# Block copies on ScalarE, clearing by memset, an earlier first load of the MoE input, and the last stores in thirds

## The chip, the cores and the metric

The kernel runs on one core of a Trainium2 chip. The time is in device microseconds (us) for one execution. The engines are TensorE (PE, its weight loads are PEld), VectorE (DVE), ScalarE (ACT), GpSimd (POOL) and SyncE (SP). Here SP issues nearly all DMA transfers; a row "SPq" in the profile is one issue on SP's queue. Each engine works through its own list of instructions in order: an instruction that waits holds everything behind it on that engine. Each DMA issue also waits until the DMA eight issues earlier has landed, because the DMAs take turns on eight semaphores (named DMAHW0 to DMAHW7 below).

## The reference

Two computations follow each other. The first is a recurrence with a 40x40 state for each of 4 batches and 8 heads, over 768 tokens; the second is a gated network with a spatial matrix.

```python
for t in range(S):                                   # S = 768, D = 40, B = 4, H = 8
    y[:, :, t] = einsum('bhd,bhde->bhe', r_t, state)
    Sa = einsum('bhde,bhe->bhd', state, a_t)
    state = state * w_t[:, :, None, :] - einsum('bhd,bhe->bhde', Sa, b_t)
    state = state + einsum('bhd,bhe->bhde', v_t, k_t)
x = y.transpose(0, 2, 1, 3).reshape(B, S, 320)
h = maximum(x @ w_in, 0)                             # 320 -> 1024
u, v = h[..., :512], h[..., 512:]
v_n = (v - mean(v)) / sqrt(var(v) + 1e-6)
v_s = einsum('ts,bsd->btd', w_spatial, v_n) + b_spatial[None, :, None]
out = (u * v_s) @ w_out                              # 512 -> 320
```

## The kernel before, in words

Phase 1 is the recurrence in chunks of C = 64 tokens. There are 24 stages: two pairs of batches, each with 12 chunks. A stage works on eight units (`NU`: two batches by four pairs of heads), and the two heads of a pair lie in the two halves of the 128 partitions (`par`). In a chunk the recurrence needs the inverse of a unit triangular 64x64 matrix; this is built from inverses of its 32x32 diagonal blocks.

Preparation of a stage q, some stages ahead of its use: the inputs `ein` are loaded in pieces (L279), DVE makes two running products (`scan1`, `scan2`, L292 to L301) and the products `at` (L318) and `sl` (L324), ACT copies a column `sc` that SP stores to DRAM (`scr`, L312), and PE multiplies the 32x32 blocks (`lprime`, L339) into a PSUM tile `bk` (128 partitions by 256). `lblock` (L349) is a DVE product of that tile with the mask `maskl`, which holds -1 above the diagonal and 0 elsewhere; the result goes to a quarter of `Lc`. Four stages (`GS`) make a group. When its four quarters stand in `Lc`, the generator `invert` turns them with a DVE transpose into `A` (L357), writes ones on the diagonal (L359), runs 30 steps of a product and an addition (L363, L367), and transposes `A` twice (L372, L374) into the tiles that the stages use. The group's inversion is spread over the four stages ahead; the first one is done in one piece before the first stage.

A stage itself is a chain over PE and ACT with short DVE pieces: `c_bp` (PE L545, copied by ACT L555 into `Rt`), `c_ff` (PE L563, reads `Rt` with the tokens' columns that a load `Rt<-in_vtok`, L384, has put there), ACT's copy `ffs` (L571), `c_xx` (PE L581, ACT L592, then POOL's masking L406), the new state `Mc` (PE L619, DVE L630), and `c_y` (PE L641, DVE L654), whose result y is stored to the DRAM buffer `xs` after every second stage (SP L666). `c_bp` of the next stage needs `Mc`, and its bank is freed by DVE's y. Beside the chain, `b_lka`, `b_tok`, `b_l21`, `b_zt` and `b_h` prepare the next stage on PE and ACT (`tk` L457, `l` L477, `zt` L496).

From stage 10 on, the first matrix product of the network runs between the stages, 128 tokens of two batches at a time. `m_load` fetches them from `xs` with six transfers (SP L685, L689), `m_u` (PE L759) and `m_v` (PE L712) multiply, and ACT and DVE finish u and v (a tile `vr`, normalised on DVE), which go to the DRAM buffers `uts` and `vns`. Phase 2 loads them, applies the spatial matrix (`spatial`, PE L179 to L181) and multiplies with w_out (`proj`, PE L199): for each half of each batch, three tiles of 128 tokens are copied by ACT (L200) into `ot`, and SP stores `ot` (L201).

The order on each engine in phase 1 is a plan written by hand. `at(t, function, arguments)` puts a call at a time t in units of stages, the calls are sorted by t, and are issued in that order; the numbers in the tables decide which instruction stands ahead of which on an engine, and nothing is reordered later, until the last stage. From there a scheduler orders what is left.

Of the kernel before, what the change touches and what calls it, by code (L numbers as in the profile page):

```python
# [18 lines left out]
P = 128  # L19
C = 64  # L20
# [81 lines left out]
def phase2(ctx, tc, marks, vns, uts, wspT, bsp, wout, out):  # L102
# [86 lines left out]
    def proj(b, h, gh, gl):  # L189
        ot = stg.tile([P, TH // P, DO], F32, name="ot")  # L190
        for j in range(TH // P):
# [9 lines left out]
        nc.sync.dma_start(  # L201
            out=out[b, h * TH:(h + 1) * TH].rearrange("(j p) n -> p j n", p=P), in_=ot
        )
# [14 lines left out]
def phase1(ctx, tc, early, late, vtok, win, xs, vns, uts, dscr):  # L218
# [125 lines left out]
    def lblock(s):  # L344
        if s % GS == 0:
            st["Lc", s // GS] = inv.tile([P, GS * NU, HB], F32, name="Lc")
        Lc = st["Lc", s // GS]
        u0 = (s % GS) * NU
        nc.vector.tensor_tensor(  # L349
            out=Lc[:, u0:u0 + NU, :], in0=st.pop(("pl", s)),  # L350
            in1=maskl.unsqueeze(1).broadcast_to([P, NU, HB]), op=ALU.mult,
        )

    def invert(g):
        Lc = st.pop(("Lc", g))
        A = inv.tile([P, HB, HB], F32, name="A")
        nc.vector.transpose(out=A, in_=Lc.rearrange("p u t -> p t u"))  # L357
        yield
# [52 lines left out]
    def b_lka_out(s, par):  # L411
        At = st["blk", s][0]
        pk = st["pk", s]
        ev = PR[1 - par]
        if s in LKA_POOL:
            nc.scalar.activation(At[par][ev], pk[ev], AF.Copy)  # L416
            strict(At[par][ev], NU)
            return
        nc.vector.tensor_tensor(
            out=At[par][ev], in0=pk[ev],  # L420
            in1=maskp[ev].unsqueeze(1).broadcast_to([64, NU, C]), op=ALU.mult,
        )
# [12 lines left out]
    def b_h_out(s, par):  # L435
        ev = PR[1 - par]
        Rt = Rts[s % 2]
        if s in H_POOL:
            nc.scalar.activation(Rt[par][ev, :, 0:C], st["ph", s][ev], AF.Copy)
            strict(Rt[par][ev, :, 0:C], NU)  # L440
            return
        nc.vector.tensor_tensor(
            out=Rt[par][ev, :, 0:C], in0=st["ph", s][ev],
            in1=maskp[ev].unsqueeze(1).broadcast_to([64, NU, C]), op=ALU.mult,
        )
# [140 lines left out]
    def c_xx_out(s, g):  # L586
# [3 lines left out]
        if s in TRI_POOL:  # L590
            for par in range(2):
                done = nc.scalar.activation(Rt[par][PR[par], gp], xx[PR[1 - par]], AF.Copy, scale=-1.0)  # L592
            marks["a", s] = done.ins
            for par in range(2):
                strict(Rt[par][PR[par], gp, 0:C], NP)
            return
        for par in range(2):
            nc.scalar.activation(Rt[par][PR[par], gp, C:], xx[PR[1 - par], :, C:], AF.Copy, scale=-1.0)
        for par in range(2):
            ur, ev = PR[par], PR[1 - par]  # L600
            nc.vector.tensor_tensor(
                out=Rt[par][ur, gp, 0:C], in0=xx[ev, :, 0:C],
                in1=maskn[ev].unsqueeze(1).broadcast_to([64, NP, C]), op=ALU.mult,
            )
# [99 lines left out]
    def m_v(g, bq, i, k=0):  # L704
# [8 lines left out]
        vr = st["act"].tile([P, DH], F32, name="vr", bufs=2)  # L713
# [65 lines left out]
    H_POOL, LKA_POOL, TRI_POOL = range(0, 99), range(0, 99), range(0, 99)  # L779
# [47 lines left out]
    SCR, SLM = {4: 0.68}, {5: 0.83}  # L827
    PREP = {4: 0.03, 5: 0.45, 6: 1.03, 7: 1.45, 8: 2.03, 9: 2.45, 10: 3.03, 11: 3.45}
    for q in range(GS, NS):
        t = PREP.get(q, q - 8 + 0.01)  # L830
        at(t + 0.20, scan1, q)
        at(t + 0.28, scan2, q)
        at(SCR.get(q, t + 0.285), scr_store, q)
        at(t + 0.29, at_mul, q, AT_ENG)
# [191 lines left out]
```

## Time and profile before

| | |
|---|---|
| three runs | 665.67, 667.46, 667.48 us (median 667.46) |
| profiled execution | 665.08 us, its span 663.3 us |
| mean granted TensorE clock | 0.943 |
| busy: PE, DVE, ACT, POOL | 571.8, 448.4, 384.2, 225.9 us |
| share of the span | 86%, 68%, 58%, 34% |

The span is the time from the first to the last event of the profile; the execution's own time is 1.8 us more. In the profile a row of a group reads: line, engine, operation, what it writes and reads, shape, count, then busy time and mean length in ns, then the idle time of the engine just before, with what ended it. A row of the timeline begins with the start in us and the length; `x4` means four instructions in a row, and the bracket gives idle time before the row and what ended it. The first stage begins at about 54 us, and the last y is stored at 491.48 us, so a stage takes some 18 us in the mean.

### The profile page before, as it was taken

The page shows a single profiled execution, that of the slowest core. Times are in us where ns is not written, and L with a number is a line of the kernel's source. Part 1 is how long each engine was busy: PE and PEld are TensorE (multiplying, and loading weights), DVE is VectorE, ACT ScalarE, POOL GpSimd, SP SyncE. Part 2 cuts the span into 40 slices and gives each one's busy share as a digit, 9 for nine tenths or more (in the row PEclk, how much of TensorE's full clock was granted, in tenths as well). Part 3 has the DMA queues.
Part 4 walks back from the last instruction along what each step waited for, and adds up shares of the span by engine and source line. Part 5 has one row for each costly group of instructions (what it writes and reads, how often), then busy time and mean ns, then how long its engine had stood idle before and what let it go on. Part 6 is the DMA issues. An engine that isn't in the chain of part 4 may idle for free.

```text
span 663.3 us, 25848 instructions
## 1 busy us (share of the span) xinstructions
PE 571.8 (86%) x10960; PEld 518.3 (78%) x10960; DVE 448.4 (68%) x970; ACT 384.2 (58%) x860; POOL 225.9 (34%) x298
## 2 busy tenths in 40 slices
PE   1447885498777887999999999999989999999997
PEld 1437674487766776888888888888878999999997
DVE  8999789989999999488896677343384842332220
ACT  2135662377666775688878887888765543221212
POOL 6013330224332334144341332332354843352221
PEclk9967997789787898999999999999998999999999
DMA  8654778477555546657565365375395557150001
GB/s 199 121 107 67 134 152 147 70 175 155 135 127 115 131 117 120 142 127 172 154 190 148 86 173 144 90 198 132 89 262 182 162 155 240 61 157 31 31 31 59
DMA packets 106331, 87.68 MB, mean 132 GB/s; under 512 B 35496, under 2 KB 92072, under 8 KB 104296
## 3 DMA queue, kind: packets, MB, share of 16 engines
q1 hardware_dynamic: 105672, 84.31, 52.0%
q10 hardware_dynamic: 544, 1.72, 1.2%
q8 instruction: 86, 1.41, 1.0%
q14 instruction: 29, 0.24, 0.1%
HBM read 59.20 MB, written 20.50 MB: 120 GB/s over the span
## 4 chain that ended last, share of the span: by engine, by line
PE 63%; DVE 15%; DMA 7%; issue 6%; ACT 4%; SPq 3%; POOL 1%; DVEq 0%; ACTq 0%; POOLq 0%
PE po L199 6%; PE pv L759 6%; PE pv L712 6%; PE pg L179 5%; PE pg L180 5%; PE pg L181 5%; PE ch L563 4%; PE bp L545 4%; PE ch L581 4%; PE bk L429 2%; DMA ein<-in_early 2%; DVE itmp L363 2%; PE bk L451 2%; PE bk L399 2%; PE bp L641 2%
## 5 line engine op out<-in xcount | busy, mean ns | idle before, releaser
L406 POOL TENSOR_SCALAR_AFFINE_SELECT Rt<-Rt 64x512 f32<-64x512 f32 (+1 forms) x144 | 83.8, 584 | 156.2 <-ACT Rt L592 128.5
L406 POOL TENSOR_SCALAR_AFFINE_SELECT At<-At 64x512 f32<-64x512 f32 x48 | 41.5, 864 | 164.0 <-ACT At L416 151.9
L555 ACT ACTIVATE Rt<-bp 64x416 f32<-64x416 f32 x96 | 49.1, 511 | 56.2 <-PE bp L545 53.6
L363 DVE TENSOR_TENSOR itmp<-A 128x30 f32<-128x30 f32 (+9 forms) x180 | 66.5, 369 | 3.4
L179 PE MATMUL pg<-wsh,vh 128*128 128x384 f32 x192 | 65.4, 341 | 2.0 <-ACT vh L51 2.0
L545 PE MATMUL bp<-lin,Mc 40*64 40x104 f32 x768 | 47.3, 278 | 22.1 <-DVE y L654 19.8
L183 DVE TENSOR_TENSOR g<-pg,bb 128x384 f32<-128x384 f32 x32 | 17.8, 556 | 70.7 <-PE pg L181 68.4
L180 PE MATMUL pg<-wsl,vh 128*128 128x384 f32 x192 | 65.1, 339 | 0.0
L181 PE MATMUL pg<-wsh,vl 128*128 128x384 f32 x192 | 63.6, 339 | 0.0
L367 DVE TENSOR_TENSOR A<-A,itmp 128x30 f32<-128x30 f32 (+9 forms) x180 | 59.1, 328 | 6.2
L545 PEld LDWEIGHTS bp<-lin,Mc 40*64 40x64 f32 x768 | 40.7, 150 | 25.5 <-DVE y L654 22.7
L563 PE MATMUL ch<-Rt,At 128*64 128x104 f32 x768 | 48.0, 283 | 5.9 <-issue 4.8
L55 POOL TENSOR_TENSOR gl<-g,gh 128x384 fp32r<-128x384 f32 x32 | 33.0, 1035 | 58.1 <-ACT gh L51 58.1
L592 ACT ACTIVATE Rt<-ch 64x416 f32<-64x416 f32 x96 | 49.1, 511 | 4.6 <-PE ch L581 2.2
L563 PEld LDWEIGHTS ch<-Rt,At 128*64 128x64 f32 x768 | 42.2, 157 | 10.4 <-issue 7.1
L51 ACT ACTIVATE gh<-g 128x384 fp32r<-128x384 f32 x32 | 16.7, 521 | 54.3 <-DVE g L184 54.3
L339 PE MATMUL bk<-at,sl 64*32 64x32 f32 x1536 | 21.2, 203 | 26.5 <-DVE sl L324 20.7
L55 POOL TENSOR_TENSOR vl<-raw,vh 128x512 fp32r<-128x512 f32 x24 | 31.5, 1324 | 31.6 <-ACT vh L51 30.1
L581 PE MATMUL ch<-ffs,xf 64*64 64x104 f32 x768 | 41.7, 261 | 0.0
L339 PEld LDWEIGHTS bk<-at,sl 64*32 64x32 f32 x1536 | 17.7, 114 | 29.5 <-issue 14.4
L179 PEld LDWEIGHTS pg<-wsh,vh 128*128 128x128 f32 x192 | 36.6, 190 | 2.4 <-ACT vh L51 2.2
L630 DVE TENSOR_TENSOR Mc<-ch,scn 104x160 f32<-104x160 f32 x44 | 18.5, 436 | 29.0 <-PE ch L619 18.7
(132 smaller groups left out, 1497.8 us busy)
## 6 DMA issues: line engine op xcount, KB each, us to landing
ein<-in_early SPq DMA_DIRECT2D x108, 129.0 KB
lin<-in_late SPq DMA_DIRECT2D x48, 160.0 KB
At<-at SPq DMA_DIRECT2D x48, 128.0 KB
uts<-ur SPq DMA_DIRECT2D x48, 128.0 KB
vns<-vr SPq DMA_DIRECT2D x24, 256.0 KB
raw<-vns SPq DMA_DIRECT2D x24, 256.0 KB
ut<-uts SPq DMA_DIRECT2D x24, 256.0 KB
Rt<-in_vtok SPq DMA_DIRECT2D x48, 80.0 KB
```

Of the source, the lines that this page charges most:

```text
L55: eng.tensor_tensor(out=lo, in0=x, in1=hi.bitcast(F32), op=ALU.subtract)
L179: nc.tensor.matmul(pg, lhsT=vh[:, dc], rhs=w_h, start=(i == 0), stop=False)
L180: nc.tensor.matmul(pg, lhsT=vh[:, dc], rhs=w_l, start=False, stop=False)
L181: nc.tensor.matmul(pg, lhsT=vl[:, dc], rhs=w_h, start=False, stop=(i == NT - 1))
L363: nc.vector.tensor_tensor(out=tp, in0=A[:, k + 1:, k:k + 1].broadcast_to([P, m, k]), in1=A[:, k:k + 1, 0:k].broadcast_to([P, m, k]), op=AL ...
L367: nc.vector.tensor_tensor(out=A[:, k + 1:, 0:k], in0=A[:, k + 1:, 0:k], in1=tp, op=ALU.add)
L406: nc.gpsimd.affine_select(out=t, in_=t, pattern=[[0, k], [1, C]], base=0, channel_multiplier=-1, compare_op=ALU.is_gt, fill=0.0,)
L545: nc.tensor.matmul(bp[PR[par], q, :], lhsT=Mc[RR[par], n, :], rhs=li[RR[par], n, C:], start=(q == 0), stop=False, skip_group_check=True,)
L555: nc.scalar.activation(Rt[par][PR[par], gp, :], st["bp", g][PR[par]], AF.Copy)
L563: nc.tensor.matmul(ff[PR[1 - par], q, :], lhsT=At[par][:, n, :], rhs=Rt[par][:, n, :], start=True, stop=True,)
L581: nc.tensor.matmul(xx[ev, q, :], lhsT=xf[ev, n, :], rhs=ffs[ev, q, :], start=True, stop=True,)
L592: done = nc.scalar.activation(Rt[par][PR[par], gp], xx[PR[1 - par]], AF.Copy, scale=-1.0)
```

## The change

It has several parts.

- `lblock` is no longer a DVE product with a mask but an ACT copy of the whole block with the factor -1 (24 instructions change engine). The part that the mask would have made zero is now copied too. In `invert`, right after the transpose, five memsets write zeros over the upper half of all blocks of the group: halves of 16x16, then 8x8, 4x4, 2x2 and single elements. They run on DVE for group 0 and on POOL for the other five groups.
- The masks `maskl`, `maskp` and `maskn` and the code that makes them on POOL at the start are gone. Branches that were never taken are dropped.
- At the start, `scr_store(q)` comes right behind the scans of its stage; before, the four came in one piece behind the loads of `At` and `ein` (six transfers, since the first stage has none).
- The tables of the plan are written in another form, mostly with the same numbers. The earliest time of the first `m_load` becomes 9.92 instead of 10.12.
- `vr` has three buffers instead of two.
- In `proj`, each of the three tiles of a result is stored right behind its copy: 24 stores of 160 KB instead of 8 of 480 KB.

```diff
@@ proj
             nc.scalar.activation(ot[:, j, :], po, AF.Copy)
-        nc.sync.dma_start(
-            out=out[b, h * TH:(h + 1) * TH].rearrange("(j p) n -> p j n", p=P), in_=ot
-        )
+            t0 = h * TH + j * P
+            nc.sync.dma_start(out=out[b, t0:t0 + P], in_=ot[:, j, :])
...
@@ lblock
-        nc.vector.tensor_tensor(
-            out=Lc[:, u0:u0 + NU, :], in0=st.pop(("pl", s)),
-            in1=maskl.unsqueeze(1).broadcast_to([P, NU, HB]), op=ALU.mult,
-        )
+        nc.scalar.activation(Lc[:, u0:u0 + NU, :], st.pop(("pl", s)), AF.Copy, scale=-1.0)
@@ invert
-        A = inv.tile([P, HB, HB], F32, name="A")
+        Af = inv.tile([P, HB * HB + HB], F32, name="A")
+        A = Af[:, 0:HB * HB].rearrange("p (t s) -> p t s", s=HB)
         nc.vector.transpose(out=A, in_=Lc.rearrange("p u t -> p t u"))
+        h = HB // 2
+        while h:
+            x = Af.rearrange("p (b x) -> p b x", x=2 * h * (HB + 1))[:, :, h:h + h * HB]
+            (nc.gpsimd if g else nc.vector).memset(x.rearrange("p b (r c) -> p b r c", c=HB)[:, :, :, 0:h], 0.0)
+            h //= 2
         yield
...
@@ m_v
-        vr = st["act"].tile([P, DH], F32, name="vr", bufs=2)
+        vr = st["act"].tile([P, DH], F32, name="vr", bufs=3)
...
@@ the plan
-    T_DEC, T_MOE = 4.2, 11
+    T_DEC, T_MOE = (4.2, 5.2, 6.2, 7.2, 8.2, 9.2), 11
...
-        at(max(own[0] - 1.6, 2 * j + 2.1, T_DEC + 5.92), m_load, bq, i)
+        at(max(own[0] - 1.6, 2 * j + 2.1, T_DEC[5] + 7 * 0.1 + 0.02), m_load, bq, i)
...
@@ the start
-        p.memset(maskl, -1.0)
-        for q in range(P // HB):
-            rows = slice(q * HB, (q + 1) * HB)
-            p.affine_select(
-                out=maskl[rows], in_=maskl[rows], pattern=[[1, HB]], base=0,
-                channel_multiplier=-1, compare_op=ALU.is_gt, fill=0.0,
-            )
...
                 scan1(q, q)
                 scan2(q)
+            scr_store(q)
             at_mul(q, v)
...
         prep_load(4, 48)
-        for q in range(GS):
-            scr_store(q)
         b_lka(0)
```

Three places show what this does to the order. On SP, where y of the stages 8 and 9 is stored (`xs<-y`), the six loads of the first `m_load` (`xt<-xs`) stood behind it before:

```order
L279 DMA ein_121<-in_early 16x2064 [waits DMAHW3_49]
L666 DMA xs<-y_3731 40x4x128 [waits DMAHW4_49,DVE_49]
L666 DMA xs<-y_3731 40x4x128 [waits DMAHW5_49]
L666 DMA xs<-y_3736 40x4x128 [waits DMAHW6_49,DVE_49]
L666 DMA xs<-y_3736 40x4x128 [waits DMAHW7_49]
L279 DMA ein_121<-in_early 16x2064 [waits DMAHW0_49]
L534 DMA scn<-scr 64x320 [waits DMAHW1_49]
L534 DMA scn<-scr 64x320 [waits DMAHW2_49]
L392 DMA At_4140<-at 64x512 [waits DMAHW3_49,PE_49,Pool_49]
L279 DMA ein_121<-in_early 16x2064 [waits DMAHW4_49]
L685 DMA xt<-xs 128x2x128 [waits DMAHW5_49]
L689 DMA xt<-xs 64x128 [waits DMAHW6_49]
```

and in the changed kernel, from the same `ein` on:

```order
L275 DMA ein_121<-in_early 16x2064 [waits DMAHW3_49]
L662 DMA xt<-xs 128x2x128 [waits DMAHW4_49]
L666 DMA xt<-xs 64x128 [waits DMAHW5_49]
L666 DMA xt<-xs 64x128 [waits DMAHW6_49]
L662 DMA xt<-xs 128x2x128 [waits DMAHW7_49]
L666 DMA xt<-xs 64x128 [waits DMAHW0_49]
L666 DMA xt<-xs 64x128 [waits DMAHW1_49]
L643 DMA xs<-y_3737 40x4x128 [waits DMAHW2_49,DVE_49]
L643 DMA xs<-y_3737 40x4x128 [waits DMAHW3_49]
L643 DMA xs<-y_3742 40x4x128 [waits DMAHW4_49,DVE_49]
L643 DMA xs<-y_3742 40x4x128 [waits DMAHW5_49]
L275 DMA ein_121<-in_early 16x2064 [waits DMAHW6_49]
```

The loads now stand ahead of the y stores; they wait for earlier DMAs alone, while the stores wait for DVE. On ACT the block copies of the changed kernel take two places in a stage. In the stages 1 to 4 one stands between the two copies `tk`:

```order
L558 ACTIVATE ffs<-ch 128x416 x2
L444 ACTIVATE tk<-bk 128x320
L345 ACTIVATE Lc<-bk 128x256
L444 ACTIVATE tk<-bk 128x320
L753 ACTIVATE xf_127<-XT_556 128x8x32
```

and all later ones, and some of these stages too, ahead of the copies of `c_bp`:

```order
L510 ACTIVATE xf_128<-bk 32x8x32 x2
L345 ACTIVATE Lc<-bk 128x256
L542 ACTIVATE Rt_131<-bp_1666 64x416
L542 ACTIVATE Rt_132<-bp_1666 64x416
L542 ACTIVATE Rt_131<-bp_1685 64x416
L542 ACTIVATE Rt_132<-bp_1685 64x416
```

Nothing else moved on ACT in these rows; the copy is new there. On POOL the five memsets of group 1 stand between the masking of `At` and that of `Rt`:

```order
L405 AFFINE_SELECT At_1303<-At_1303 64x512
L355 MEMSET A 128x16x16
L355 MEMSET A 128x2x8x8
L355 MEMSET A 128x4x4x4
L355 MEMSET A 128x8x2x2
L355 MEMSET A 128x16
L405 AFFINE_SELECT Rt_129<-Rt_129 64x4x64
```

The memsets wait for the group's transpose on DVE. Of DVE's instructions only the transposes at the end of the inversion wait for the memsets.

More of the change, by code (lines that the diff above doesn't have):

```diff
@@ L254, in phase1 @@
     eseg = ends.rearrange("p (n c) -> p n c", c=WSEG)
-    maskl = const.tile([P, HB], F32, name="maskl")
     ident = const.tile([P, P], F32, name="ident")
-    maskp = const.tile([P, C], F32, name="maskp")
-    maskn = const.tile([P, C], F32, name="maskn")
     Mc = const.tile([P, NU, C], F32, name="Mc")
@@ L414, in b_lka_out @@
         ev = PR[1 - par]
[L415 to L421, printed above, removed]
-        )
+        nc.scalar.activation(At[par][ev], pk[ev], AF.Copy)
+        strict(At[par][ev], NU)
     def b_h(s):
@@ L437, in b_h_out @@
         Rt = Rts[s % 2]
[L438 to L445, printed above, removed]
+        nc.scalar.activation(Rt[par][ev, :, 0:C], st["ph", s][ev], AF.Copy)
+        strict(Rt[par][ev, :, 0:C], NU)
     def b_tok(s, h):
@@ L589, in c_xx_out @@
         xx = st["xx", g]
[L590 to L596, printed above, removed]
         for par in range(2):
-            nc.scalar.activation(Rt[par][PR[par], gp, C:], xx[PR[1 - par], :, C:], AF.Copy, scale=-1.0)
+            done = nc.scalar.activation(Rt[par][PR[par], gp], xx[PR[1 - par]], AF.Copy, scale=-1.0)
+        marks["a", s] = done.ins
         for par in range(2):
[L600 to L604, printed above, removed]
+            strict(Rt[par][PR[par], gp, 0:C], NP)
     def c_mp(s, g):
@@ L778, in phase1 @@
     AT_ENG, SL_ENG, LO_ENG, XC = v, v, p, act_copy
-    H_POOL, LKA_POOL, TRI_POOL = range(0, 99), range(0, 99), range(0, 99)
     M1, M2, M3, M4 = 0.22, 0.46, 0.65, 0.80
@@ L852, in phase1 @@
         for k in range(8):
-            at(T_DEC + i + k * 0.10 - (0.9 if k == 0 else 0), step, gen)
-    at(T_DEC + 5.9, open_act)
+            at(T_DEC[i] + k * 0.1 - (0.9 if k == 0 else 0), step, gen)
+    at(T_DEC[5] + 7 * 0.1 + 0.01, open_act)
     slots = [T_MOE + k // 4 + (M1, M2, M3, M4)[k % 4] for k in range(3 * NS)]
@@ L890, in phase1 @@
         pads(v, ein[1])
-        p.memset(maskl, -1.0)
-        for q in range(P // HB):
-            rows = slice(q * HB, (q + 1) * HB)
-            p.affine_select(
-                out=maskl[rows], in_=maskl[rows], pattern=[[1, HB]], base=0,
-                channel_multiplier=-1, compare_op=ALU.is_gt, fill=0.0,
-            )
         pads(p, ein[2])
@@ L905, in phase1 @@
         make_identity(nc, ident)
-        for m, val in ((maskp, 1.0), (maskn, -1.0)):
-            p.memset(m, val)
-            for rows in PR:
-                p.affine_select(
-                    out=m[rows], in_=m[rows], pattern=[[1, C]], base=0,
-                    channel_multiplier=-1, compare_op=ALU.is_gt, fill=0.0,
-                )
         for t in (Mc, *xfs):
```

28 lines of the change are left out of this document (15 added, 13 removed).

## The prediction

> **What bounds the kernel now.** I read the table of stretches first, because the 68% of DVE and 86% of PE in the page's first part average over stages with different limits. Its columns are the stretch and its length, then busy time of PE, PEld, DVE, ACT and POOL, then granted TensorE clock, DMA share and GB/s.
>
> ```profile
> 14.00:54.00 40.00, 18.09 (x453) 16.48 (x455) 37.07 (x82) 11.45 (x28) 4.17 (x6) 0.77 0.59 110
> 54.00:84.60 30.60, 26.64 (x822) 23.26 (x818) 22.94 (x32) 19.90 (x48) 12.61 (x14) 0.91 0.68 116
> 84.60:147.00 62.40, 42.02 (x1214) 37.06 (x1208) 57.78 (x113) 32.17 (x75) 14.78 (x22) 0.84 0.69 134
> 147.00:257.00 110.00, 90.45 (x2604) 79.92 (x2606) 106.02 (x215) 77.54 (x176) 38.52 (x53) 0.91 0.57 129
> 257.00:264.00 7.00, 2.46 (x30) 1.93 (x26) 6.72 (x14) 2.69 (x7) 2.14 (x2) 0.77 0.95 129
> 264.00:366.00 102.00, 101.45 (x2368) 88.82 (x2366) 77.91 (x183) 80.31 (x185) 33.79 (x51) 0.98 0.61 154
> ```
>
> From 14 to 54 DVE is 37.07 of 40 us busy (scans, then the whole inversion of group 0). From 54 to 84.6 no engine is full. From 84.6 to 257 DVE is 163.8 of 172.4 us busy: it is the bound, and every DVE operation taken out there is worth its own length. From 257 to 264 PE works 2.46 of 7 us. After 264 PE is 99% busy, and nothing taken from DVE can pay. The waits of 54 to 135 (total, times, longest) say the same: PE's c_bp stands still for y on DVE.
>
> ```profile
> PE bp L545 <- DVE y L654: 8.3, 2, 4.5
> ```
>
> **The 24 block copies (L349) go from DVE to ACT.** On DVE one takes 0.42 us; ACT's nearest copies out of the bank, larger and narrower than the new 128x256, are the next two rows.
>
> ```profile
> L349 DVE TENSOR_TENSOR Lc<-bk,maskl x24: 410/419/426, 14.7 to 351.3; 128x256 f32<-128x256 f32 x24
> L457 ACT ACTIVATE tk<-bk 128x320 f32<-128x320 f32 x48 | 19.7, 435 | 8.0 <-PE bk L451 7.6
> L477 ACT ACTIVATE l<-bk 32x256 f32<-32x256 f32 x48 | 18.0, 375 | 8.3 <-PE bk L468 7.4
> 140.96 0.42 DVE L349 TENSOR_TENSOR Lc<-bk,maskl 128x256 f32<-128x256 f32 x1 [0.94 <-PE bk L339]
> 147.07 0.44 DVE L630 TENSOR_TENSOR Mc<-ch,scn 104x160 f32<-104x160 f32 x1 [1.40 <-ACT Rt L592]
> ```
>
> I take 0.40 us on ACT. Twelve of the 24 copies, those of stages 7 to 18, lie between 84.6 and 257, and DVE starts its next operation about 0.34 us after one. Five of them come before 147.07, 5 x 0.34 = 1.7 us (the fifth, at 140.96, had DVE wait 0.94 us for PE too). But there Mc waited 1.40 us for ACT's Rt, so what DVE wins only lengthens this wait, unless the work of PE and ACT ahead of it moves forward too. It does in part, since PE's c_bp waits for DVE's y; against it ACT has a copy of 0.40 us more, between two tk copies. I take 1.0. The next six stand in gapless DVE work: 6 x 0.34 = 2.1 us (the twelfth comes behind the y that counts below). Together **-3.1 us** by 257. Bounds: 5 (twelve copies at 0.34 and the wait of 0.94) and nothing (each 0.34 us turns into a wait for a load). In 54 to 84.6 I count none: three copies lie there, but DVE then waits for loads or stores, as at 84.63, right behind the last.
>
> ```profile
> 84.63 1.26 DVE L292 TENSOR_TENSOR_SCAN S<-ein,ends 128x528 f32<-128x528 f32 x1 [0.96 <-DMA scr<-sc]
> 297.72 2.12 ACT L555 ACTIVATE Rt<-bp 64x416 f32<-64x416 f32 x4 [1.34 <-PE bp L545]
> ```
>
> After 264 the copy stands ahead of Rt<-bp on ACT. At 297.72 ACT had waited 1.34 us for PE's c_bp, and on PE the lprime matmuls that fill the bank stand ahead of that c_bp: the copy fits into this idle time. Price there 0; without that cover 0.40 us for each of five copies.
>
> **The clearing memsets.** Nothing in the trace has their strided shape. They clear 256, 128, 64, 32 and 16 elements a partition; the rows bracket them by size:
>
> ```profile
> L881 DVE MEMSET ein<- 128x512 f32 x1 | 0.5, 485 | 0.0
> L359 DVE MEMSET A<- 128x32 f32 x6 | 0.5, 85 | 0.0
> L881 POOL MEMSET ein<- 128x512 f32 x2 | 1.0, 522 | 0.1
> L907 POOL MEMSET maskp<- 128x64 f32 x1 | 0.1, 146 | 0.0
> ```
>
> A line through the DVE rows gives about 0.27, 0.17, 0.11, 0.09 and 0.07: 0.7 us for group 0, on DVE (bounds 0.4 and 2.4, five times each end). On POOL the five make about 0.9 us (0.7 to 2.6), behind the group's transpose. They hold only POOL's next affine_select, and DVE's last transposes, some 20 or more us later. At the second group's transpose POOL is idle:
>
> ```profile
> 94.01 0.49 POOL L406 TENSOR_SCALAR_AFFINE_SELECT Rt<-Rt 64x256 f32<-64x256 f32 x1 [5.08 <-ACT Rt L592]
> 25.56 0.42 DVE L349 TENSOR_TENSOR Lc<-bk,maskl 128x256 f32<-128x256 f32 x1 [0.44 <-PE bk L339]
> 26.02 1.94 DVE L357 STREAM_TRANSPOSE A<-Lc 128x1024 f32<-128x1024 f32 x1
> ```
>
> At the start two earlier copies leave DVE's way to the last lprime (2 x 0.34 us); the transpose at 26.02 then starts about 0.6 us earlier, and the memsets give 0.7 back: **0** (-0.6 to +1.8). The scr stores moved ahead, and At and ein(4) moved behind six of them, lie under the inversion, which holds all to 54; the mask building that POOL loses lies ahead of it. The dropped branches were never taken.
>
> The Trainium skill has a rule that bears here: SBUF — State Buffer, "Who interferes with whom", says that a DVE instruction with two SBUF inputs collides with a GpSimd instruction that reads SBUF, not with one that only writes. By it the memsets cost the inversion steps beside them nothing, and the sum stays; without it, 0.9 us of memsets in each of five groups could stretch DVE by up to 4.5 us, and the sum would be that much poorer. No run so far shows a memset beside a step.
>
> **The first loads of xs (m_load) move up on SP.** Now SP stands before xs<-y(9) until DVE has y, 236.47 to 241.44, and only behind it come six xt loads.
>
> ```profile
> 235.40 1.07 SPq L279 DMA_DIRECT2D ein<-in_early  x2
> 241.44 1.56 SPq L666 DMA_DIRECT2D xs<-y  x4
> 246.20 0.41 SPq L685 DMA_DIRECT2D xt<-xs  x1
> 249.84 1.12 SPq L689 DMA_DIRECT2D xt<-xs  x2
> 257.08 0.58 SPq L384 DMA_DIRECT2D Rt<-in_vtok  x1
> 258.05 0.52 PE L759 MATMUL pv<-xh,wl 128*128 128x256 f32 x3
> 261.99 0.58 PE L563 MATMUL ch<-Rt,At 128*64 128x104 f32 x2 [3.42 <-issue]
> 263.68 3.00 PE L563 MATMUL ch<-Rt,At 128*64 128x104 f32 x30 [1.12 <-DMA Rt<-in_vtok]
> 257.08 6.47 DMA Rt<-in_vtok
> ```
>
> From 241.44 SP issues without a pause to the second vtok at 257.08; it lands 6.47 us later, at 263.55, and c_ff(11), which could start at about 258.57, runs only then: 5.1 us. The six loads take 246.20 to 250.96, 4.76 us of SP. In the change they stand ahead of xs<-y(9), and wait for earlier DMAs alone, so they fall into SP's idle 4.97 us. Everything behind, vtok included, is issued about 4.7 us earlier: **-4.6 us** (bounds -5.1, the whole wait, and 0, if landing is what limits: the DMA share of 257 to 264 is 0.95). It adds to the 3.1 because SP's row starts from ein issues that wait for DVE to free their buffer; if it didn't, both together would give 4.7.
>
> **PE's clock behind that wait.** The next rows have the columns of the first table.
>
> ```profile
> 264.00:265.00 1.00, 1.00 (x16) 1.00 (x14) 1.00 (x1) 0.00 (x0) 0.00 (x0) 0.50 0.68 177
> 268.00:270.00 2.00, 2.00 (x50) 1.82 (x50) 0.00 (x0) 1.18 (x4) 0.00 (x0) 1.00 0.42 96
> 243.68 1.92 PE L563 MATMUL ch<-Rt,At 128*64 128x104 f32 x32
> ```
>
> The granted clock is 0.50 behind the idle time and 1.00 again at 268. Thirty matmuls of c_ff take 3.00 us there, where 32 took 1.92 at 243.68. A short wait would save this 1.2 us; I take **-1.0** (0 to -1.7).
>
> The Trainium skill, TensorE: Matmul & The Clock Gate, "Part 1: The HAM clock gate (the "warmup" mystery)", says that an idle window of about 3.4 us halves the clock, and as long a busy one restores it. The trace agrees: 3.42 us of idle, then 0.50 until 268. No row shows the shortest wait that costs the clock; by the rule the term is -1.2 for a wait under 3.4 us, and 0 for one above it.
>
> **Third vr buffer.** At 489.89 ACT's vr waits 0.75 us for the store of an older vr, and 1.95 us of PE hang behind.
>
> ```profile
> 489.89 0.60 ACT L714 ACTIVATE vr<-itmp 128x512 f32<-128x512 f32 x1 [0.75 <-DMA vns<-vr]
> 498.57 0.44 PE L179 MATMUL pg<-wsh,vh 128*128 128x384 f32 x1 [1.95 <-ACT vh L51]
> ```
>
> Between them stand SP's stores and loads (xs<-y, raw<-vns), so I pass on half of the 0.75: **-0.4** (0 to -1.95).
>
> **The stores in thirds.** Every proj result is stored as three pieces, 24 issues instead of 8. SP waits there for ACT (81.2 us, below), so the 16 added issues of 0.37 us cost nothing. Only the last store counts.
>
> ```profile
> SPq L201 <- ACT ot L200: 81.2, 6, 17.3
> 659.26 0.44 ACT L200 ACTIVATE ot<-po 128x320 f32<-128x320 f32 x1 [1.32 <-PE po L199]
> 659.72 0.37 SPq L201 DMA_DIRECT2D out_y<-ot  x1
> 660.80:661.20 0.40, 0.00 (x0) 0.00 (x0) 0.00 (x0) 0.00 (x0) 0.00 (x0) 1.00 1.01 358
> ```
>
> At 358 GB/s 480 KB move in about 1.4 us and a third in 0.47: **-0.95** (0 to -1.1).
>
> The Trainium skill speaks against splitting: DMA: Bandwidth & Descriptors, "Anatomy of one DMA — SWDGE (gpsimd) path", gives 2.0 us plus bytes over 436 GB/s for each DMA. As an estimate the last third then takes 2.4 us against 3.1, a gain of 0.75; the sum would be 0.2 us poorer, since the first two pieces go out beside PE's work. The row gives 3.6 us from issue at 659.72 to the end of the span at 663.3.
>
> **The sum.** -3.1 - 4.6 - 1.0 - 0.4 - 0.95 = -10.05 us. The terms hang in one chain of due times, and what one frees may meet the next wait, so I keep 9 of the 10. The profiled execution took 665.08 us (span 663.3): 656.1. The runs' median, 667.46, is 2.4 above it, so I forecast **658.5**.
>
> **The rivals.** (A) The transfer is hidden no better: vtok is issued earlier, but lands late since DMA is full (share 0.95). Against it: the six loads leave the crowded time for one in which SP now issues nothing. Then -3.1 - 0.4 - 0.95 = -4.45: **663.0**. (B) DVE's gain turns into waits for loads on SP's row, and vtok stays: only the tail is left, -1: **666.5**, the same. For it speaks 54 to 84.6; against it DVE's 96% in 147 to 257. (C) Slower: ACT becomes what the stage loop waits for. Its copies stand in order ahead of Rt<-bp, tk and ffs; if lprime on PE ends later than c_bp, ACT is held with Rt<-bp ready behind it, and PE with it. Price: 20 copies behind the start x 0.40 = 8.0, less the 1.35 of tail and vr, +6.6: **674**. It decides from the point where ACT's wait for c_bp is under 0.40 us; now it is 0.56 a copy in the mean (53.6 us over 96, below), but most comes in few long waits. ACT is 79% busy from 264 to 366 and gets to about 81%.
>
> ```profile
> L555 ACT ACTIVATE Rt<-bp 64x416 f32<-64x416 f32 x96 | 49.1, 511 | 56.2 <-PE bp L545 53.6 <-POOL xl L55 0.7 <-issue 0.2
> ```
>
> **How the numbers follow.** Forecast 0.58, A 0.24, B 0.11, C 0.07. A measurement here tells about 0.3%, 2.0 us, from no change. The forecast and A lie beyond that bound: faster 0.82, same 0.11, slower 0.07. The likeliest's own range is 654 (the best bounds of the two large terms and the clock, -13.2) to 661 (DVE's term at nothing, -7); with A and 2 us above it the range becomes **654 to 665**, leaving out B and C.
>
> **What would show it.** Right: no L349-like operation on DVE; the waits of PE's c_bp for y shorter; the DVE-bound stretch shorter by 3 us; the six xt issues ahead of xs<-y(9); vtok issued near 250, c_ff(11) waiting under 2 us and a clock of 1.00 behind it; the span's end 2.7 us behind the last ot. Wrong: ACT Lc holding Rt<-bp with PE waiting (C); vtok's landing over 8 us after its issue (A); new DVE waits for ein or scr (B).

## The result, and the profile after

The changed kernel took 662.52 us (median of 16 runs, 658.51 to 667.07), the kernel before 667.19 us (16 runs on the same chip, 660.87 to 669.38). The ratio is 0.9948 with a 95% interval of 0.9926 to 0.9971: **3.5 us faster (1.9 to 4.9), where 9.0 were forecast.** The medians lie 4.7 us apart and the means 3.5 (666.25 and 662.75); the ratio and its interval are those of the means. The direction was right; the size was less than half of the forecast.

One profiled execution of each hides this. That of the changed kernel took 664.58 us (span 662.9), that of before 665.08: half a microsecond apart, the one above its kernel's median, the other below. Runs of one kernel spread by more than 8 us here, so the ratios below come from many runs, and what a profile shows is read in several.

The table of stretches of the changed kernel, with the columns of the prediction's first one:

```profile
14.00:54.00 40.00, 18.27 (x454) 16.48 (x444) 36.31 (x83) 12.76 (x32) 3.98 (x6) 0.86 0.61 109
54.00:84.60 30.60, 26.81 (x702) 23.53 (x698) 20.76 (x27) 20.09 (x49) 11.72 (x14) 0.80 0.73 111
84.60:147.00 62.40, 41.02 (x1165) 36.72 (x1160) 52.77 (x101) 29.32 (x68) 12.73 (x23) 0.78 0.58 119
147.00:257.00 110.00, 91.45 (x2506) 80.31 (x2508) 103.49 (x201) 80.69 (x185) 36.67 (x60) 0.89 0.64 136
257.00:264.00 7.00, 5.50 (x212) 4.74 (x214) 6.66 (x19) 4.98 (x11) 5.34 (x8) 1.00 0.89 142
264.00:366.00 102.00, 101.94 (x2350) 89.64 (x2348) 81.84 (x186) 83.58 (x192) 36.32 (x60) 0.98 0.62 155
```

From 84.6 to 257 DVE is now 156.3 us busy of 172.4, against 163.8 before. The window is fixed in time, so this says only that DVE idles more. The work itself did not come earlier: y(9), the y of stage 9, ended at 248.18 us, against 241.75 before (247.7 and 244.0 in a second profile of each). The groups of the changed kernel name the wait (the transposes and copies of all six groups, then the memsets):

```profile
L351 DVE STREAM_TRANSPOSE A<-Lc 128x1024 f32<-128x1024 f32 x6 | 11.7, 1951 | 11.3 <-ACT Lc L345 11.3
L345 ACT ACTIVATE Lc<-bk 128x256 f32<-128x256 f32 x24 | 9.2, 382 | 19.1 <-PE bk L335 18.9
L355 DVE MEMSET A<- 128x256 f32 x1 | 0.3, 272 | 0.1
L355 DVE MEMSET A<- 128x16 f32 x1 | 0.1, 72 | 0.0
L355 POOL MEMSET A<- 128x256 f32 x5 | 1.6, 312 | 26.9 <-DVE A L351 26.9
```

A copy takes 0.382 us on ACT (0.40 forecast), and the memsets cost what was worked out (0.27 to 0.07 us on DVE). But DVE stands 11.3 us ahead of the six transposes, waiting for ACT's copies; before, the transposes waited 0.2 us in all, and the products ahead of them 5.5 us for PE (the same groups of the kernel before):

```profile
L357 DVE STREAM_TRANSPOSE A<-Lc 128x1024 f32<-128x1024 f32 x6 | 11.8, 1964 | 0.2
L349 DVE TENSOR_TENSOR Lc<-bk,maskl 128x256 f32<-128x256 f32 x24 | 10.1, 419 | 5.5 <-PE bk L339 5.5
```

In the timeline of the changed kernel the second and third group have most of it. Below the two transposes stand ACT's copies ahead of them, and PE's lprime ahead of the first of these copies:

```profile
95.16 1.95 DVE L351 STREAM_TRANSPOSE A<-Lc 128x1024 f32<-128x1024 f32 x1 [5.23 <-ACT Lc L345]
148.34 1.97 DVE L351 STREAM_TRANSPOSE A<-Lc 128x1024 f32<-128x1024 f32 x1 [3.47 <-ACT Lc L345]
94.75 0.38 ACT L345 ACTIVATE Lc<-bk 128x256 f32<-128x256 f32 x1 [0.54 <-PE bk L335]
147.93 0.38 ACT L345 ACTIVATE Lc<-bk 128x256 f32<-128x256 f32 x1
93.58 1.08 PE L335 MATMUL bk<-at,sl 64*32 64x32 f32 x64
```

The profile names ACT, but most of this is a wait for PE. For the second group lprime ends at 94.66, and ACT, which had been idle for 0.54 us, copies at 94.75. For the third group lprime ends at 146.98, and ACT comes to the copy 0.95 us later, behind `ffs` and a `tk`. Over all six groups 7.8 of the 11.3 us pass before lprime has ended and 3.5 behind it. Other profiles agree on the second part only: with all copies in these places on ACT, DVE waits 7.7 to 11.3 us in five profiles, 3.3 to 4.5 of it behind lprime; with the product on DVE it waits 5.1 to 11.1 us in five, for PE. So what is new is ACT's part, some 3 to 4 us, and the pair of profiles shown here makes the rest look larger than it is.

The loads of `xs` and vtok, on SP and PE of the changed kernel:

```profile
243.06 0.43 SPq L662 DMA_DIRECT2D xt<-xs  x1
245.33 2.07 SPq L666 DMA_DIRECT2D xt<-xs  x2
247.87 1.86 SPq L643 DMA_DIRECT2D xs<-y  x4
258.47 0.59 SPq L383 DMA_DIRECT2D Rt<-in_vtok  x1
268.33 1.65 PE L550 MATMUL ch<-Rt,At 128*64 128x104 f32 x32
```

All six loads are issued by 247.40, ahead of the y stores. vtok is issued 10.6 us behind the y stores' start, against 15.6 before: the move does what it should. c_ff(11) no longer waits for it (the last row has no wait), and the clock from 257 to 264 is 1.00. At the end, SP's last store and ACT's last copy:

```profile
659.74 0.44 ACT L200 ACTIVATE ot<-po 128x320 f32<-128x320 f32 x1 [1.32 <-PE po L199]
660.20 0.33 SPq L202 DMA_DIRECT2D out_y<-ot  x1
```

The span ends 2.69 us behind the last copy (660.18), against 3.65 before.

### The profile page after: what moved, and what is told of

Read it like the earlier page. It is cut to its first block, busy times and chain, and to the rows that moved or that the text cites. A ratio compares the mean times of both kernels' runs of the same rounds, so it can differ in the third digit from the quotient of the medians.

```text
span 662.9 us, 25888 instructions
## 1 busy us (share of the span) xinstructions
PE 577.4 (87%) x10960; PEld 523.0 (79%) x10960; DVE 445.2 (67%) x951; ACT 394.3 (59%) x884; POOL 225.2 (34%) x312
## 4 chain that ended last, share of the span: by engine, by line
PE 67%; DVE 13%; issue 7%; ACT 5%; DMA 5%; SPq 2%; POOL 1%; DVEq 0%; ACTq 0%; POOLq 0%
PE po L199 6%; PE pv L736 6%; PE pv L689 6%; PE pg L179 5%; PE pg L181 5%; PE pg L180 5%; PE bp L532 5%; PE ch L550 4%; PE ch L568 4%; PE bk L422 3%; PE bk L438 3%; DVE itmp L362 3%; PE bk L398 3%; DMA ein<-in_early 3%; DVE A L366 2%
## 5 line engine op out<-in xcount | busy, mean ns | idle before, releaser
L362 DVE TENSOR_TENSOR itmp<-A 128x30 f32<-128x30 f32 (+9 forms) x180 | 68.7, 382 | 3.5
L532 PE MATMUL bp<-lin,Mc 40*64 40x104 f32 x768 | 47.7, 280 | 16.7 <-DVE y L631 14.2
L51 ACT ACTIVATE gh<-g 128x384 fp32r<-128x384 f32 x32 | 16.7, 522 | 54.5 <-DVE g L184 54.5
L568 PE MATMUL ch<-ffs,xf 64*64 64x104 f32 x768 | 43.2, 267 | 0.0
L568 PEld LDWEIGHTS ch<-ffs,xf 64*64 64x64 f32 x768 | 38.3, 144 | 1.1
```

Of the source, the lines that this page charges most:

```text
L362: nc.vector.tensor_tensor(out=tp, in0=A[:, k + 1:, k:k + 1].broadcast_to([P, m, k]), in1=A[:, k:k + 1, 0:k].broadcast_to([P, m, k]), op=AL ...
L532: nc.tensor.matmul(bp[PR[par], q, :], lhsT=Mc[RR[par], n, :], rhs=li[RR[par], n, C:], start=(q == 0), stop=False, skip_group_check=True,)
L568: nc.tensor.matmul(xx[ev, q, :], lhsT=xf[ev, n, :], rhs=ffs[ev, q, :], start=True, stop=True,)
```

## The experiments

All ratios are against the kernel before on the same chip in the same batch; the changed kernel has 0.9948 in two batches.

| kernel | ratio | 95% interval |
|---|---|---|
| block part alone | 0.9979 | 0.9947 to 1.0011 |
| first m_load alone | 0.9962 | 0.9932 to 0.9991 |
| stores in thirds and third vr alone | 0.9978 | 0.9953 to 1.0003 |
| changed, block part undone | 0.9936 | 0.9905 to 0.9966 |
| before, DVE product three times | 1.0160 | 1.0123 to 1.0197 |
| changed, ACT copy three times | 1.0044 | 1.0015 to 1.0073 |
| changed, four copies moved | 1.0028 | 1.0003 to 1.0053 |
| changed, no copies | 0.9900 | 0.9854 to 0.9946 |
| changed, PE kept busy | 1.0024 | 0.9988 to 1.0061 |
| changed, m_load at its old place | 1.0001 | 0.9970 to 1.0032 |
| changed, again | 0.9948 | 0.9913 to 0.9984 |
| changed, one copy moved | 0.9950 | 0.9921 to 0.9979 |
| changed, one copy on DVE | 0.9970 | 0.9931 to 1.0009 |
| changed, eight copies on DVE | 0.9959 | 0.9927 to 0.9991 |

### The parts one by one

The block part alone, on the kernel before. The scr stores at the start move with it; in the old order ACT would wait for itself.

```diff
-        nc.vector.tensor_tensor(out=Lc[...], in0=..., in1=maskl..., op=ALU.mult)
+        nc.scalar.activation(Lc[...], ..., AF.Copy, scale=-1.0)
@@ invert: the five memsets; @@ start: no maskl, scr_store(q) behind scan2(q)
```

> The kernel before with the block part alone: lblock on ACT, clearing memsets, no maskl, and the scr stores moved ahead at the start (ACT would otherwise wait for itself there). As predicted (theory 1): -3 us, and the end of y(9) 2 to 3 us earlier than the 241.75 of before. Theory 2 (the block copies cost in stages 1 to 4, since ACT frees the bank later than DVE did and PE then idles and loses its clock): +3 to +6 us, with y(4) 4 to 7 us later than the 151.77 of before. Theory 3 (the 6.6 us that the changed kernel had lost by y(4) in its one profile are chance of that execution: code loads and the clock): within 2 us of before.

Measured: -0.21% (-1.4 us, between -3.5 and +0.7). y(4) ends at 154.8 us in its profile and y(9) at 243.7, neither as theory 1 nor as theory 2 has it, but one profile decides little here. The time excludes theory 2's +3 to +6 and leaves theory 1 (-3) and theory 3 (within 2).

The first m_load alone:

```diff
-        at(max(own[0] - 1.6, 2 * j + 2.1, T_DEC + 5.92), m_load, bq, i)
+        at(max(own[0] - 1.6, 2 * j + 2.1, 9.92), m_load, bq, i)
```

> The kernel before with the first m_load at 9.92 alone. As predicted: -5.6 us (wait for vtok 4.6, clock 1.0), and c_ff(11) waits under 2 us. Rival A of the prediction: the load lands as late as before, 0 to -1 us. By the step of the changed kernel's profile between y(9) and y(11): -3.6 us.

Measured: -0.38%, -2.5 us (-4.5 to -0.6). c_ff(11) does not wait at all; the gain is under half of the 5.6.

The two edits at the end, together:

```diff
-        nc.sync.dma_start(out=out[b, h * TH:(h + 1) * TH]..., in_=ot)
+            nc.sync.dma_start(out=out[b, t0:t0 + P], in_=ot[:, j, :])
-        vr = st["act"].tile([P, DH], F32, name="vr", bufs=2)
+        vr = st["act"].tile([P, DH], F32, name="vr", bufs=3)
```

> The kernel before with the stores in thirds and three vr buffers alone. As predicted: -1.35 us (0.95 at the last store, 0.4 for vr). By the changed kernel's profile, whose stretch from the last y to the end is 3.5 us shorter: -3 us. The distance from the last ot to the span's end should fall from 3.6 to about 2.7 us in any case.

Measured: -0.22%, -1.5 us, with an interval that just reaches no change. The distance from the last `ot` to the end is 2.69 us in its profile. In all 17 profiles it is 2.68 to 2.70 with the stores in thirds and 3.65 to 3.67 without: 0.96 us, as forecast.

The changed kernel with the block part undone:

```diff
-        nc.scalar.activation(Lc[...], ..., AF.Copy, scale=-1.0)
+        nc.vector.tensor_tensor(out=Lc[...], in0=..., in1=maskl..., op=ALU.mult)
@@ invert: no memsets; @@ start: maskl made again
```

> The changed kernel with the block part undone (lblock on DVE with its mask, no memsets); all else as changed. Theory 1: 3 us slower than the changed kernel, that is about -1 us or no change against before. Theory 2: 3 to 6 us faster than the changed kernel, -7 to -10 us against before. Theory 3: like the changed kernel, -3.5 us against before.

Measured: -0.64% (-0.95 to -0.34), not distinguishable from the changed kernel's -0.52%. So with the rest in place the block part is worth about 0.8 us to the worse, and alone 1.4 to the better: **nothing, within 2 us either way.** It bears out theory 3; theory 1 (about no change against before) and theory 2 (-7 to -10 us) lie outside this interval.

### What a DVE product and an ACT copy cost

If both engines had idle time there, adding work would tell. First the kernel before, with the product done three times in the stages 4 to 23:

```diff
+        for _ in range(3 if s >= GS else 1):
             nc.vector.tensor_tensor(out=Lc[...], in0=pl, in1=maskl..., op=ALU.mult)
```

> The kernel before with the block product on DVE done three times over for the stages 4 to 23 (the two added ones write the same values): 40 more DVE operations of 0.34 to 0.42 us. If every DVE operation between 84.6 and 257 is worth its length, as the prediction had it, the 24 added there cost 8 to 10 us, and those behind 264 nothing: +8 to +10 us. If DVE's saving did not pay because DVE is the bound for a part of the time only, clearly less: 0 to +4 us.

Measured: +1.60%, **+10.6 us** for 40 added products (+8.2 to +13.1). The group of the product:

```profile
L351 DVE TENSOR_TENSOR Lc<-bk,maskl 128x256 f32<-128x256 f32 x64 | 27.0, 422 | 6.5 <-PE bk L339 5.1
```

In its profile 26 of the added products lie ahead of y(9), 11.0 us at 0.422, and y(9) ends at 253.2 us, against 241.8 to 245.5 in the four profiles in which these stages are the kernel before's. From there to the last y it takes 245.7 us, against 244.5 to 248.2. So the loss lies in the stretch where DVE is full, and the products behind it cost nothing. PE's wait for y, which the prediction had named as the sign of the bound, does not show it (from 54 to 265, first in this kernel, then in the kernel before):

```profile
PE bp L547 <- DVE y L656: 16.2, 8, 2.6
```

```profile
PE bp L545 <- DVE y L654: 19.8, 11, 4.5
```

So a DVE operation that is added there is paid nearly in full. The prediction took from the full busy share that one removed is won in full; that does not follow.

The changed kernel with the copy done three times:

```diff
+        for _ in range(3 if s >= GS else 1):
             nc.scalar.activation(Lc[...], pl, AF.Copy, scale=-1.0)
```

> The changed kernel with the block copy on ACT done three times over for the stages 4 to 23: 40 more ACT copies of 0.38 us. If the copies lie in ACT's idle time (the prediction): 0 to +2 us against the changed kernel (-3.5 to -1.5 against before). If one copy already stands on the path (rival C, or the waits of tk and Rt behind it in stages 1 to 4): up to 15 us, and more than 4 in any case, so slower than before.

Measured: +0.44% against before, +0.96% or 6.4 us against the changed kernel, for 40 copies that take 15.4 us. The added copies lie partly on the path, and in the profile (of the quickest of its runs) DVE's wait at the transposes is longer:

```profile
L353 DVE STREAM_TRANSPOSE A<-Lc 128x1024 f32<-128x1024 f32 x6 | 11.8, 1975 | 13.9 <-ACT Lc L347 13.9
```

Last, no copies at all behind the start. This kernel leaves out part of the work: groups 1 to 5 invert the block tile of group 0 again.

```diff
     def lblock(s):
+        if s >= GS:
+            st.pop(("pl", s))
+            return
...
-        Lc = st.pop(("Lc", g))
+        Lc = st["Lc", 0]
```

> The changed kernel without the block copies of the stages 4 to 23: the groups 1 to 5 invert the block tile of group 0 again, so the result is not the reference's; the matmuls, memsets and inversions stay. If the ACT copies cost what doubling them suggests (40 added ones cost +0.96% against the changed kernel, 6.4 us): 3 us faster than the changed kernel. If they lie in idle time and only added ones beyond that hurt: within 1 us of it. Against the changed kernel with the blocks still on DVE (-0.64% against before), the tripled DVE product (+10.6 us for 40) would have it 5 us faster.

Measured: 0.9900, 3.2 us faster than the changed kernel; all six of its runs (653.6 to 657.6 us) lie below the median of the changed kernel beside it (660.5). The wait at the transposes is gone but for the first group.

```profile
L354 DVE STREAM_TRANSPOSE A<-Lc 128x1024 f32<-128x1024 f32 x6 | 11.8, 1959 | 1.2 <-ACT Lc L348 1.2
```

The 3.2 us come out as worked out from the tripled copy (6.4 us for 40, so 3.2 for 20). The intervals of the two kernels are wide (0.9854 to 0.9946 and 0.9913 to 0.9984), and neither way isolates the copies: without them the transposes wait no longer for PE's lprime either, and tripling tells what a second and a third copy cost, not the first. But the two agree: **the 20 copies behind the start cost up to about 3 us, and this is the likeliest place where DVE's saving goes.** Against the block product on DVE (0.9936) no copies win 2.4 us, with intervals that overlap.

### Where on ACT

First, lprime and the copies of stages 5, 7, 9 and 11 behind the `l` copies, so that none stands between the two `tk` (in stage 2 the copy had stood ahead of both, behind `ffs`, and not between them as the order above has it):

```diff
-    LPQ = {}
+    LPQ = {5: 1.07, 7: 1.07, 9: 1.07, 11: 1.07}
-    INV_T = {1: (2.5, 3.7), 2: (4.5, 7.7), ...}
+    INV_T = {1: (2.58, 3.7), 2: (4.58, 7.7), ...}
```

> The changed kernel with lprime and the block copy of the stages 5, 7, 9 and 11 moved behind the l copies, so that no block copy stands between the two tk copies on ACT; the inversion of the groups 1 and 2 is set 0.08 stages later to come behind them. If the second tk, held up by the bank that ACT frees late (0.53 us in stage 1 of the changed kernel's profile), cost time in the stages 1 to 4: 1 to 3 us faster than the changed kernel. If not: within 1 us of it.

Measured: +0.28%, 5 us worse than the changed kernel. Stage 1 became shorter (from y(0) to y(1) 16.3 us, against 20.3 in the changed kernel's profile), stage 4 longer (24.8 against 18.8), with a wait of PE for which the profile names no cause, and DVE's Mc behind it (waits of that kernel from 135 to 161):

```profile
DVE Mc L607 <- ACT Rt L431: 4.3, 1, 4.3
PE bk L422 <- issue: 4.3, 1, 4.3
```

This wait stands at matmul 2504 of PE's list and is one of the stops of the last section, longer than any other; whether the 5 us of the other runs have to do with it, one profile can't tell.

Read over the profiles, stage 1 was 14.8 to 19.1 us in six with the product on DVE and 19.0 to 21.1 in six with the copy between the two `tk`. Three runs were to settle whether that place is the loss: the copy of stage 5 alone moved (`LPQ = {5: 1.07}`), that copy alone on DVE, and the copies of stages 4 to 6 and 19 to 23 on DVE.

```diff
+        if s == 5:                    # third kernel: s in (4, 5, 6) or s > 18
+            nc.vector.tensor_scalar(out=Lc[...], in0=pl, scalar1=-1.0, scalar2=None, op0=ALU.mult)
+        else:
             nc.scalar.activation(Lc[...], pl, AF.Copy, scale=-1.0)
```

> The changed kernel with lprime(5) and its block copy alone moved behind the l copies of stage 1 (of the four moved together before, which made stage 1 shorter, 16.3 us, and stage 4 6 us longer). If the copy between the two tk copies is what makes stage 1 long (19.0 to 21.1 us in six profiles with it there, 14.8 to 19.1 in six with the product on DVE): stage 1 under 18 us, stage 4 still 18 to 19 us, 3 us faster than the changed kernel, -0.9% against before. If not: stage 1 over 19 us and -0.5%.

> The changed kernel with the block copy of stage 5 alone done on DVE (as a product with -1, no mask), in the same place of the plan. If ACT's in-order place between the tk copies costs: as the run above, stage 1 under 18 us and -0.9% against before. If stage 1 is long for another reason that the ACT kernels share (the copy of stage 4 ahead of Rt<-bp, or the order at the start): stage 1 over 19 us and -0.5%.

> The changed kernel with the block copies of the stages 4 to 6 and 19 to 23 done on DVE, where DVE has idle time, and those of 7 to 18 on ACT, where DVE is full. If the ACT copies cost in stages 0 to 4 (+4 us) and win 1.4 us in stages 5 to 9, as the profiles so far read: 4 us faster than the changed kernel, -1.0 to -1.2% against before, faster than each kernel so far that does all the work. If the costs of ACT's copies lie elsewhere: -0.5 to -0.7%.

Measured: -0.50%, -0.30% and -0.41%. Stage 1 is 15.0, 17.5 and 19.0 us in the three profiles, so the first two changed it as expected. The third did too: stage 1 also holds 0.5, 3.3 and 3.9 us of the stops of the last section, and without them it is 14.5, 14.2 and 15.1 us, against 17.3 to 17.7 in the six profiles with the copy between the two `tk`. Yet none of the three is faster than the changed kernel. The reading fails: what stage 1 wins is not kept in the time of the whole. Which of the copies make the 3 us stays open, and the mixed version does not beat the changed kernel. None of the kernels that do all the work was shown to be faster than it; the best value, 0.9936 with the block part undone, lies within its interval.

### vtok and m_load

The kernel before once more, for its profile:

> The kernel before once more, for a second profile of it. If the 5.1 us wait for vtok at c_ff(11) belongs to the kernel, it is there again. If it belonged to one execution (y(9) came at 241.75 us there, and at 243.7 to 248.2 in the five other profiles), it is under 1.5 us, as in the profile with only the ends changed (0.8 us), and y(9) comes near 245.

The execution took 661.76 us, and the 5.1 us are not there. In its waits of PE from 240 to 275, and in those of the kernel with the block part alone from 240 to 268 (both with the loads at their old place):

```profile
PE ch L563 <- DMA Rt<-in_vtok: 0.4, 1, 0.4
```

```profile
PE ch L565 <- DMA Rt<-in_vtok: 0.2, 1, 0.2
```

The changed kernel with m_load at its old place (the floor 10.12 again):

```diff
-        at(max(own[0] - 1.6, 2 * j + 2.1, T_DEC[5] + 7 * 0.1 + 0.02), m_load, bq, i)
+        at(max(own[0] - 1.6, 2 * j + 2.1, 10.12), m_load, bq, i)
```

> The changed kernel with the first m_load at its old place behind the y stores of the stages 8 and 9. As predicted: 5.6 us slower than the changed kernel. If the wait for vtok is the accident of one profile: 0 to 2.5 us slower, no wait over 1.5 us at c_ff(11), and y(9) to y(10) longer by about 1 us.

Measured: 1.0001, 0.53% or 3.5 us slower than the changed kernel beside it. vtok is waited for 1.3 us:

```profile
263.61 1.61 PE L550 MATMUL ch<-Rt,At 128*64 128x104 f32 x30 [1.28 <-DMA Rt<-in_vtok]
```

With the run of m_load alone (-2.5 us) its worth is about 3 us. Over the six profiles with the loads at their old place c_ff(11) waited 4.5, 0.4, 0.8, 0.2, 1.6 and 1.3 us, in the mean 1.5; in the eleven with them moved it did not wait. The rest of the 3 us was not traced to a wait.

### The clock

PE kept busy with 112 matmuls whose results nobody uses, where it waits for DVE in the stages 2 to 10:

```diff
+    def warm_pe(n):
+        pv = ps_m.tile([P, DH], F32, name="pv")
+        for _ in range(n):
+            nc.tensor.matmul(pv[:, 0:P], lhsT=ident, rhs=ident, start=True, stop=True)
+    for s, n in {3: 16, 4: 14, 5: 8, ..., 10: 8}.items():
+        at(s - 0.003, warm_pe, n)
...
```

> The changed kernel with 112 more 128x128 matmuls on PE, results unused, in places where PE waits for DVE in the stages 2 to 10 (ahead of c_bp, and two places in stage 3). They take 0.14 us each at full clock. If the clock of 0.50 that follows PE's waits is on the path (some 50 us of the stretch from 54 to 265 were granted 0.50 in each profile): 2 to 6 us faster than the changed kernel, and less than half of that half-clock time left. If PE's speed there is covered by DVE, or the matmuls come too late to hold the clock: no change to +4 us.

And the changed kernel again, beside it:

> The changed kernel once more, to stand beside the three above on the same chip and for a second profile of it: -0.5% against before, and y(4) nearer to 155 than to the 158.18 us of its first profile, if the early loss there was chance.

Measured: 1.0024 and 0.9948. The stretch from 54 to 265, first of the changed kernel, then with the added matmuls:

```profile
54.00:265.00 211.00, 164.34 (x4660) 144.50 (x4656) 185.45 (x349) 136.82 (x315) 68.37 (x103) 0.87 0.62 127
```

```profile
54.00:265.00 211.00, 183.35 (x4844) 162.80 (x4843) 186.14 (x354) 136.08 (x315) 63.68 (x104) 0.93 0.63 129
```

The granted clock rises from 0.87 to 0.93 (the time at 0.50 falls from 55 to 30 us), and the kernel is 5 us slower. Buying the clock with PE's time doesn't pay here. In the second profile of the changed kernel y(4) came at 158.1 us again, not near 155 as expected; so the early lateness may belong to it more than I took it to after the first batch. With m_load at its old place, which leaves these stages as they are, it came at 155.7. The total is still 3.5 us better than before.

## Why the prediction was right or wrong, point by point

| step | forecast | measured |
|---|---|---|
| start | 0 | -0.3 and -0.6 us in two pairs of profiles (last transpose of group 0 at 51.88 and 52.91, before 52.17 and 53.48) |
| block copies, 84.6 to 257 | -3.1 | 0, within 2 us |
| vtok and PE's clock behind it | -5.6 | -2.5 and -3.5 (two ways) |
| third vr buffer, stores in thirds | -1.35 | -1.5 together |
| all | -9.0 | -3.5 (-1.9 to -4.9) |

**The step that failed most is the one on vtok.** "c_ff(11), which could start at about 258.57, runs only then: 5.1 us" was read from one execution and taken for the kernel. The mechanism was right: the six issues fall into SP's idle time, and vtok goes out some 4 us earlier behind y(9) (9.8 to 11.1 us against 14.1 to 14.4; 15.3 in the execution that I had). The amount was not: in five other profiles with the loads at their old place the wait was 0.2 to 1.6 us. In the profile that I had, both sides of the race lay badly. Counted from y(9), PE was ready for c_ff(11) after 16.8 us, in the five others after 17.3 to 18.9; and the matmuls that need the second vtok ran after 21.9 us, in the others after 18.9 to 20.1. PE was early because stage 10 was quick (13.7 us, with a clock of 1.00 in its c_bp; 13.7 to 15.4 in the others), and vtok was late because SP issued it a us later and it took 6.5 us to land, 4.7 to 5.9 in four of the others.

The clock's term of 1.0 hung on that wait and went with it. Its reading "3.42 us of idle, then 0.50" was also too simple: PE had been idle for only 2.16 us when the clock fell, as the next rows of the kernel before show (columns as in the table of stretches). So a shorter wait can cost the clock too.

```profile
258.57:260.73 2.16, 0.00 (x0) 0.00 (x0) 2.06 (x6) 1.17 (x4) 1.81 (x2) 1.00 1.06 137
260.73:261.99 1.26, 0.00 (x1) 0.03 (x1) 1.26 (x2) 0.00 (x0) 0.33 (x1) 0.50 1.04 136
```

**The block copies failed at "every DVE operation taken out there is worth its own length".** Rows of DVE that are busy without a gap show what an added operation costs, and the tripled product bore that out (10.6 us for 40). What a removed one wins is bounded by the next thing that DVE needs. Here that is the group's transpose: it needs the fourth block, for which DVE waits on PE's lprime and, behind it, on ACT's copy. In the profile DVE waits 11.3 us at six transposes where it had waited 5.7 at products and transposes together. The prediction had no term for this wait: ahead of the third group's transpose it took off 0.7 for Mc's wait for ACT, and at the second, where 5.23 us arise, it took off nothing. That no gain is left is measured (within 2 us); that it went into these waits and into the time that ACT's copies cost, at most about 3 us, is read from the profiles and from two runs that do not isolate it. Rival C, ACT in the way, was thus true in part, at up to 3 us rather than the 8 of its price, and not enough to end on its side.

**Right** were ACT's copy (0.382 us for 0.40), the memsets (0.71 us on DVE for 0.7; on POOL 0.93 for 0.9, sum of the five kinds' means), the start within its bounds, and the last store (0.96 us for 0.95). On the stores the Trainium skill's formula (DMA: Bandwidth & Descriptors, "Anatomy of one DMA — SWDGE (gpsimd) path") would have given 0.75, by a fit for DMAs that GpSimd issues; the row of what the DMA moved was nearer. The rule that memsets on POOL leave DVE alone (the Trainium skill, SBUF — State Buffer, "Who interferes with whom") is not contradicted by these runs: a step's product took 382 ns in the mean against 369, but 369 to 383 over the profiles with memsets and 367 to 373 over those without (394 with the tripled product), and no run here separates the memsets from POOL's other work.

**The vr term** was a wait that went away, and nothing else. ACT no longer waits for the store in any profile with three buffers (with two it waited in three of five), but PE's wait for `vh` behind it is 1.1 to 2.5 us with three and 0.6 to 2.0 with two. I find no gain of it; the 1.5 us of the two edits is 0.96 for the store and a rest within the interval.

**The range** held the time, but only because A had widened it: the likeliest's own range ended at 661. That the time lies beside A's 663.0 is luck, since A's reason, a vtok that lands as late as before, did not occur: c_ff(11) waited for it in none of the eleven profiles with the loads moved. The sum should have been cut first for resting on one execution.

## What to carry to other kernels

A wait in one profile is a sample: where two chains race to one instruction (here vtok by SP, and y by DVE), take a second profile of the unchanged kernel before pricing it. An engine that is busy without a gap tells what more work on it costs; for what less is worth, name the instruction on it that will wait next, and what stands ahead of its producer on the other engine, and then what that producer itself waits for. Tripling the work on the old engine, tripling it on the new one and leaving it out bound the price from three sides; leaving it out also removes the waits for what the work reads.

## What the runs showed of the hardware

**PE stops at the same instructions, whatever the kernel, and waits there for its code.** In three profiles its wait in the middle of c_ff(2), with nothing to wait for in the profile, stands at the same matmul but for one: 0.56 us and 0.83 in the two of the kernel before, 2.57 in the changed kernel.

```profile
86.82 1.23 PE L563 MATMUL ch<-Rt,At 128*64 128x104 f32 x22 [0.56 <-issue]
```

```profile
88.88 1.23 PE L563 MATMUL ch<-Rt,At 128*64 128x104 f32 x22 [0.83 <-issue]
```

```profile
92.45 1.20 PE L550 MATMUL ch<-Rt,At 128*64 128x104 f32 x21 [2.57 <-issue]
```

Counted over PE's list, such places stand at the matmuls 856, 982, 1236, 1362, 1744, 2633 and 2759: the distances are 126, 254, 126, 382, 889 and 126, all near multiples of 127. The one at 1744, give or take one, is there in all 17 profiles, 1.25 to 3.21 us long. The page of the kernel before lists, by packets, MB and share of the DMA engines' time:

```profile
q8 instruction: 86, 1.41, 1.0%
```

These are 86 packets of 16 KB, and 86 times 127 is 10,922, nearly all of PE's 10,960 matmuls. The trace has the time of each packet. From 54 to 265 us the 17 profiles hold 145 stops of PE of over 0.4 us at which it has nothing to wait for in the profile, and each ends 1.2 to 2.3 us behind the landing of such a packet, 142 of them 1.1 to 2.1 us behind. Of 267 equally long waits whose end the profile explains, only one in six lies so. As far as the traces tell, then, PE waits at these places for its next piece of code. The longest stop, the 4.3 us in the kernel with four copies moved, began at 149.14, before its packet was even on the way (150.01 to 151.41). Why a piece comes late, perhaps because loads crowd the DMA, was not tested.

In this stretch the stops make 9.4 us of the kernel before's profile, 16.6 of the changed kernel's, and 6.5 to 16.7 over all. They differ between profiles by up to 10 us, where the whole change won 3.5, which is a reason why the length of a stage in one profile misleads.

**The clock goes in steps of 3.4 us, and about half a step of idle time is enough to halve it.** The granted clock is 0.50 or 1.00, in stretches of 3.4 us and multiples, and where these fall differs between executions of one kernel. Between 54 and 480 us the 17 profiles have 138 falls and 155 rises of the clock. In the 3.4 us before a fall PE was, by the profile, busy for 0 to 59% of the time; in the 1683 steps at 1.00 that no fall followed, for 51 to 100%; before a rise, for 84 to 100%. So PE need not be idle for a whole step to lose the clock, and has to be busy for nearly a whole one to get it back. Stage 10 took 13.6 to 13.9 us in the six profiles with a clock of 1.00 in its c_bp, and 14.8 to 16.3 in the seven with 0.50 or 0.51. How much of the 8 us by which runs of one kernel differ comes from this, and how much from the stops above, was not measured.
